# A fused attention and MLP kernel: query transposes of the third batch moved from the DMA engines to TensorE, and a denser order in the first batch

## The chip, the cores and the metric

The kernel runs on one core of one Trainium2 chip. The core has a matrix engine (TensorE, PE in the profile, its weight loads PEld), a vector engine (VectorE, DVE), an activation engine (ScalarE, ACT), a general engine (GpSimd, POOL) and a synchronisation engine (SyncE, SP), and it shares 16 DMA engines among all of its transfers. The metric is the time of one execution on the device in microseconds (us). The kernel before took 806.96 us as the median of three runs (805.3 to 807.57); the execution that was profiled took 805.28 us, of which the profile covers a span of 803.5 us.

## The reference

The reference is grouped attention followed by a residual MLP. Eight batches have 384 positions, 16 query heads, 4 key and value heads and a head size of 64, so that the model width is 1024 and the hidden width 4096.

```python
scores = (1 / 8) * q @ k.T            # per batch and query head, k shared by 4 heads
attn   = softmax(scores)              # over the keys
x      = attn @ v                     # put together as [batch, 384, 1024]
a1     = alpha1 * x + beta1
tok    = w_tok @ a1                   # 384 x 384, mixes positions
u      = x + lam * tok
a2     = alpha2 * u + beta2
out    = u + lam * (relu(a2 @ w_ch1) @ w_ch2)      # 1024 -> 4096 -> 1024
```

All inputs and the output are float32. The kernel rounds what goes through TensorE to bfloat16.

## The kernel before: the parts that matter

The eight batches run as a pipeline. `main(b)` is the MLP of batch b. It has two passes: the first (`h`) computes the hidden layer, 32 blocks of 8 matmuls, and streams the first weight matrix from memory in 16 tiles of two blocks each; the second (`ch`) multiplies by the second weight matrix, which stays on the chip. `side(b + 1)`, the attention and token mixing of the next batch, is woven into the matmuls of `main(b)`, mostly into its second pass. The first batch has nobody's MLP to hide behind: its `side(0)` runs alone at the head of the kernel, in a hand-written order.

Each batch needs its keys and queries turned, with the head dimension on the partitions (`kT`, `qT`). Two means exist for this. A *flip* is a transposing DMA from one on-chip buffer to another. A *turn* is a TensorE transpose into PSUM, and a copy of the result by VectorE.

```python
def flip_queue(b):
    return nc.scalar if b == 2 else nc.sync

def flip_k(b):                                  # 12 blocks of 128 x 128
    flip_queue(b).dma_start_transpose(out=kT..., in_=k2s[b]...)

def flip_q(b, i=0, n=NP):                       # n pairs of heads: 3 n blocks
    flip_queue(b).dma_start_transpose(out=qT[:, i:i + n]..., in_=qrs[b][:, 2 * i:2 * (i + n)]...)
...
def load_w1(n):                                 # one tile of the first weight matrix
    t = sb.tile([P, NDT, CW * P], bf, tag="w1", name="w1", bufs=RING)      # RING = 5
    nc.gpsimd.dma_start(out=t, in_=w1src[...])
...
def q_transpose(p, n=2, tag="tp", eng="DVE"):   # a turn of n pairs: 3 n transposes, one copy
    src = qrs[1][:, 2 * p:2 * (p + n)] if b else qgs[...]
    ps = bank([P, n * NST, P], tag, "tp", src.dtype)
    for i in range(n * NST):
        nc.tensor.matmul(out=ps[:, i, :], lhsT=src[:, i * P:(i + 1) * P], rhs=..., is_transpose=True, ...)
    evac(eng)(out=qT[:, p:p + n]..., in_=ps)
```

Batches are counted from 0, so the third batch is `b == 2`. Its keys and queries are flipped while the first pass of `main(1)` runs, and the flips are issued from ScalarE's queue. All later batches are flipped from SyncE's queue during a second pass. In the first pass ScalarE also empties every second block of hidden units from PSUM (the even `nt`; VectorE takes the odd ones), and TensorE has two PSUM banks for these blocks (tag `mm`).

```python
# main(b), first pass, for each of 16 weight tiles and each of its two blocks nt
ps = bank([P, 512], "mm", "h")                  # two banks in turn
for dt in range(NDT):
    nc.tensor.matmul(out=ps[:, :n], lhsT=w1[:, dt, ...], rhs=a2T[:, dt, :n], ...)
    if dt == 3: yield 0                         # a place where side work may come in
if nt % 2 == 0:
    nc.scalar.activation(out=hT[:, nt, :], in_=ps[:, :S], func=RELU, bias=c1)
else:
    nc.vector.tensor_scalar(out=hT[:, nt, :], in0=ps[:, :S], ...)
yield 0                                         # so two places a block, 64 in the pass
...
load_w1(b * NCH + c + RING)                     # when tile c is used up, tile c + 5 is asked for
```

```python
moves = []                                      # (pass, place, what)
if b == 1:
    moves = [(0, 46 + 4 * i, flip_q, 2, 2 * i - 2, 2) if i else (0, 46, flip_k, 2) for i in range(5)]
```

In the first batch beta1 has to enter the token mixing through a product of two small matrices (`R` and `H`), since the sum `alpha1 * x + beta1` is not formed there. `R` is made of row sums of `w_tok` (`rows_r`), `H` of beta1 times lam, split into three bfloat16 parts so that nothing is lost in rounding (`scale_rows(1)`, `split(1, 2)`, then `fill_h`). All of this runs on VectorE.

```python
def split(lo, hi, step=None):
    for i, m in enumerate(masks[:2]):
        nc.vector.tensor_copy(out=rows_b[:32, c], in_=src[:, c])
        nc.vector.scalar_tensor_tensor(out=dst[:, c], in0=rows_b[:32, c], scalar=m, in1=src[:, c], op0=MUL, op1=subtract)
    nc.vector.tensor_copy(out=rows_b[:32, c], in_=rows_f[:, c])
...
at = {...                                       # after scores(i), for i in 0 to 17
      4: [(av, 0)], 5: [(wtok_transpose, 0, "av"), (wtok_transpose, 1, "tp")],
      6: [(av, 1), (wtok_transpose, 2, "av"), (k_transpose, 2, 2, "tp")],
      7: [(q_transpose, 4, 2, "av"), (scale_rows, 1), (split, 1, 2)],
      8: [(fill_h, 0), (rows_r, "tp"), (av, 2)], 9: [(spread, upper, ...), (q_transpose, 6, 2, "mm")],
      10: [(tok, 0)], 11: [(av, 3)], 12: [(tok, 1), (ut, 0)], 13: [(av, 4), (tok, 2)], ...
```

Here `scores(i)` are the score matmuls, each followed by an exponential on ScalarE; `av(p)` multiplies by the values for head pair p, after which VectorE normalises (a reciprocal and a product into `x`) and multiplies by alpha1 (`a1`); `tok(p)` is the token mixing, `ut(p)` the transpose of u for the MLP. `av`, `tok` and one of the query turns take the two `mm` banks in turn.

Of the kernel before, what the change touches and what calls it, by code (L numbers as in the profile page):

```python
# [12 lines left out]
def kernel(  # L13
# [21 lines left out]
    nc = tc.nc  # L35
    f32 = mybir.dt.float32
# [2 lines left out]
    RELU = mybir.ActivationFunctionType.Relu  # L39
    MUL = mybir.AluOpType.mult  # L40
    ADD = mybir.AluOpType.add

    B, Hq, S, D = q.shape
    Hkv = k.shape[1]
    G = Hq // Hkv
    DM = Hq * D
    DFF = moe_w_ch1.shape[1]
    P = 128
# [65 lines left out]
        for h in range(0, Hq, G):  # L114
            nc.gpsimd.dma_start(out=qrs[b][:, h:h + G], in_=q[b, h:h + G].rearrange("h (p st) d -> p h st d", st=NST))

    def flip_queue(b):
        return nc.scalar if b == 2 else nc.sync

    def flip_k(b):  # L120
        flip_queue(b).dma_start_transpose(out=kT.rearrange("p st h s -> p (st h) s"),
                                    in_=k2s[b].rearrange("p st h a d -> p (st h a d)"))

    def flip_q(b, i=0, n=NP):
        flip_queue(b).dma_start_transpose(out=qT[:, i:i + n].rearrange("p a j s -> p (a j) s"),
                                    in_=qrs[b][:, 2 * i:2 * (i + n)].rearrange("p h st d -> p (h st d)"))

    w1src = moe_w_ch1.rearrange("(dt di) nf -> di dt nf", di=P)
# [12 lines left out]
        nc.gpsimd.dma_start(out=w2[:, r, cs], in_=w2src[:, r, cs])  # L141

    def bank(shape, tag, name, dtype=f32):
        if tag == "mm":
            return mms.tile(shape, dtype, tag="mm", name=name, bufs=2)
        return psum.tile(shape, dtype, tag=tag, name=name, bufs=2 if tag == "sc" else 1)

    def three():
        return threes[0].tile([P, 2, 4, P], f32, tag="sc", name="sc", bufs=3)

    def tp_ps(shape, tag="tp"):
        return bank(shape, tag, "tp", bf)
# [21 lines left out]
    def side(b):  # L174
# [8 lines left out]
        def cols(p):  # L183
            return slice(p * P, (p + 1) * P)

        def bc(t, p):
            return t[:, None, cols(p)].to_broadcast([P, NST, P])
# [7 lines left out]
                                  in_=ps.rearrange("p (h st) s -> p h st s", h=n))  # L195

        def q_transpose(p, n=2, tag="tp", eng="DVE"):
            src = qrs[1][:, 2 * p:2 * (p + n)] if b else qgs[2 * p // G][:, 2 * p % G:2 * p % G + 2 * n]
            src = src.rearrange("p h st d -> p (h st d)")
            f = src.dtype == f32  # L200
            ps = bank([P, n * NST, P], tag, "tp", src.dtype)
            for i in range(n * NST):
                nc.tensor.matmul(out=ps[:, i, :], lhsT=src[:, i * P:(i + 1) * P], rhs=ident_f if f else ident,  # L203
                                 is_transpose=True, start=(i == 0), stop=(i == n * NST - 1), skip_group_check=True)
            evac(eng)(out=qT[:, p:p + n].rearrange("p a j s -> p (a j) s"), in_=ps)
# [33 lines left out]
        def av_piece(p, hh):  # L239
            if hh == 0:  # L240
                if first:
                    avs[p] = bank([P, 2, NST, D1], "mm", "av")
                else:
                    avs[p] = three()[:, 0].rearrange("p k s -> p (k s)")[:, :2 * NST * D1].rearrange(
                        "p (h st d) -> p h st d", h=2, st=NST)
            av = avs[p]
            hk = (2 * p + hh) // G
            for sq in range(NST):
                m = NST * hh + sq
                for sk in range(NST):  # L250
                    k = (p * NST + sk) * NST + m // 2
                    nc.tensor.matmul(out=av[:, hh, sq, :], lhsT=ess[k // 4][:, m % 2, k % 4, :],  # L252
                                     rhs=vb[:, sk, hk, :], start=(sk == 0), stop=(sk == NST - 1))
            if hh == 0:
                return
            rinv = sb.tile([P, 2, NST, 1], f32, tag="rinv", name="rinv", bufs=1)
            nc.vector.reciprocal(out=rinv, in_=av[:, :, :, D:])  # L257
            nc.vector.tensor_tensor(out=x[:, :, cols(p)].rearrange("p st (h d) -> p h st d", h=2), in0=av[:, :, :, :D],  # L258
                                    in1=rinv.to_broadcast([P, 2, NST, D]), op=MUL)
            if first:  # L260
                a1s[p] = hTf[:, 6144 + p % 3 * S:6144 + (p % 3 + 1) * S].rearrange("p (a d) -> p a d", a=NST)
                nc.vector.tensor_tensor(out=a1s[p], in0=x[:, :, cols(p)], in1=bc(g1, p), op=MUL)
                return
            t = sb.tile([P, NST, P], f32, tag="tmp", name="a1f", bufs=4)
            nc.vector.tensor_tensor(out=t, in0=x[:, :, cols(p)], in1=bc(g1, p), op=MUL)  # L265
            a1s[p] = sb.tile([P, NST, P], bf, tag="a1", name="a1", bufs=2)
            nc.vector.tensor_tensor(out=a1s[p], in0=t, in1=bc(h1, p), op=ADD)  # L267

        def tok(p):
            ps = bank([P, NST, P], "mm", "tok") if first else three()[:, 0, :NST]  # L270
# [78 lines left out]

        if not first:  # L350

            turns = {}
            if b == 1:
                turns = {4: [(split, 2, 4, 0)], 8: [(split, 2, 4, 1)], 12: [(k_transpose, 0)],
                         16: [(q_transpose, 0, 2, "av")], 20: [(k_transpose, 2)]}
                for i in range(3):
                    turns[24 + 4 * i] = [(q_transpose, 2 + 2 * i, 2, "av")]
                for i in range(4):
                    turns[34 + 4 * i] = [(spread, (2 * i, 2 * i + 1), (1, 3), "tp", "ACT")]
                for i in range(2):  # L360
                    turns[50 + 4 * i] = [(spread, range(4 * i, 4 * i + 4), (3, 4), "av", "ACT")]
            return turns, {
                0: [(scores3, 0)], 4: [(av, 0)], 6: [(scores3, 1)], 8: [(tok_flip, 0)], 11: [(av, 1)],
                13: [(scores3, 2, True)], 15: [(av, 2)], 16: [(tok_flip, 1)], 18: [(tok_flip, 2)], 19: [(av, 3)],
                21: [(scores3, 3)], 23: [(tok_flip, 3)], 25: [(av, 4)], 27: [(scores3, 4)], 29: [(tok_flip, 4)],
                31: [(av, 5)], 33: [(scores3, 5, True)], 35: [(av, 6), (tok_flip, 5)], 37: [(av, 7)],
                39: [(tok_flip, 6)], 41: [(tok_flip, 7)]}
# [5 lines left out]
        ut = a2_transpose  # L373
        at = {0: [(warmup, 3), (scale_rows, 0), (split, 0, 1, 0)], 1: [(k_transpose, 1, 1), (split, 0, 1, 1)],
              2: [(q_transpose, 2, 2, "av")], 3: [(warmup, 1), (spread, lower, (0, 1), "tp")],
              4: [(av, 0)], 5: [(wtok_transpose, 0, "av"), (wtok_transpose, 1, "tp")],
              6: [(av, 1), (wtok_transpose, 2, "av"), (k_transpose, 2, 2, "tp")], 7: [(q_transpose, 4, 2, "av"), (scale_rows, 1), (split, 1, 2)],
              8: [(fill_h, 0), (rows_r, "tp"), (av, 2)], 9: [(spread, upper, (0, 1), "av", "ACT"), (q_transpose, 6, 2, "mm")],
              10: [(tok, 0)],
              11: [(av, 3)], 12: [(tok, 1), (ut, 0)], 13: [(av, 4), (tok, 2)], 14: [(ut, 1), (fill_h, 4), (tok, 3)],  # L380
              15: [(av, 5), (ut, 2)], 16: [(tok, 4), (ut, 3)], 17: [(av, 6), (tok, 5)]}
        for i in range(18):
            add(scores, i)
            for f, *a in at.get(i, []):
                add(f, *a)
        for f, *a in ((ut, 4), (h_part, (0, 1), range(4)), (av, 7), (ut, 5), (tok, 6),
                      (h_part, (2, 3), range(4)), (h_part, range(4), (4,)), (ut, 6), (tok, 7),
                      (h_part, range(4), (5,)), (ut, 7), (h_part, range(4), (6,)), (h_part, range(4), (7,))):
            add(f, *a)
        return us  # L390
# [64 lines left out]
    with tc.manual_schedule(engines=order):  # L455
# [59 lines left out]
                nc.vector.tensor_reduce(out=t[:n], in_=ident[:n, :n].rearrange("p (k c) -> p c k", c=NP), op=ADD, axis=AX)  # L515


        def scale_rows(i):
            r = rows_f[:, i * P:(i + 1) * P]
            nc.vector.tensor_tensor(out=r, in0=r, in1=rows_f[:, 3 * P:4 * P], op=MUL)  # L520


        def split(lo, hi, step=None):
            c = slice(lo * P, hi * P)
            for i, m in enumerate(masks[:2]):
                if step in (None, i):
                    src, dst = (rows_t, rows_f) if i else (rows_f, rows_t)
                    nc.vector.tensor_copy(out=rows_b[:32, c], in_=src[:, c])
                    nc.vector.scalar_tensor_tensor(out=dst[:, c], in0=rows_b[:32, c], scalar=m, in1=src[:, c],
                                                   op0=MUL, op1=mybir.AluOpType.subtract)  # L530
            if step != 0:
                nc.vector.tensor_copy(out=rows_b[:32, c], in_=rows_f[:, c])


        def fill_h(p):
# [2 lines left out]
                                    in1=sel4[:, p:p + 4, None].to_broadcast([32, 4, P]), op=MUL)  # L538

        load_v(0)  # L540
        nc.gpsimd.dma_start(out=wtok_in, in_=moe_w_tok.rearrange("(p tt) s -> p tt s", tt=NST))
        load_q4(2)
        load_q4(3)
        place_k(0, 0, (0,))
        for c in range(RING):
            load_w1(c)
        place_k(0, 1)

        load_k(1)
        load_q(1)  # L550
# [7 lines left out]
        load_k(2)  # L558
        for b in range(B):
            us = side(b + 1) if b + 1 < B else ({}, {})  # L560


            moves = []
            if b == 1:
                moves = [(0, 46 + 4 * i, flip_q, 2, 2 * i - 2, 2) if i else (0, 46, flip_k, 2) for i in range(5)]
            if 0 < b < B - 2:
                moves += [(1, 1, load_k, b + 2), (1, 2, load_next, b + 2), (1, 34, flip_k, b + 2), (1, 36, flip_q, b + 2, 0, 2),
                          (1, 37, flip_q, b + 2, 2, 2), (1, 42, flip_q, b + 2, 4, 2), (1, 43, flip_q, b + 2, 6, 2)]
# [38 lines left out]
```

The softmax here doesn't subtract the row's maximum and nothing guards it: scores larger than these inputs give would overflow.

## Time and profile before

The profile is that of one execution. Idle time of an engine counts only if it holds up the engine that sets the end.

| What | Before |
|---|---|
| time, median of three runs | 806.96 us (805.3 to 807.57) |
| profiled span | 803.5 us |
| VectorE busy | 343.5 us (43%) |
| ScalarE busy | 226.9 us (28%) |
| GpSimd busy | 178.5 us (22%), 112.1 us of it in issuing the w_ch1 loads |
| tiles of w_ch1, issue to landing | 128, 512 KB each |
| flips of queries on ScalarE's queue | 4, 13.0 us from issue to landing |
| flips of queries on SyncE's queue | 20, 2.8 us from issue to landing (median) |

A line of the timeline gives the start and the length of a group of instructions, the engine, the line of the kernel, what is written and read with its shape, the number of instructions, and in square brackets the time for which the engine stood idle before it and what ended that wait. Engine letters with a q (ACTq, SPq) are the engine's sequencer, which issues DMAs. Lengths of neighbouring matmuls overlap, because they are pipelined; how long a piece of TensorE work really takes is read from the distance between starts.

### The profile page before, as it was taken

Reading aid. Unit: us, or ns where it says so; the run is one execution under the profiler, and the core shown is the slowest. Engines: PE = TensorE matmul, PEld = TensorE weight load, DVE = VectorE, ACT = ScalarE, POOL = GpSimd, SP = SyncE. Lnnn points to the kernel's source line nnn. Section 1 sums busy time; section 2 is a strip of 40 time slices with the busy share of each in tenths; the row PEclk is TensorE's granted clock in tenths of the full one; section 3 lists DMA queues with packets and bytes.
Section 4 is the critical chain, followed back from the end, with each engine's and each line's share of the span. In section 5 each row is a group of like instructions: output and inputs, shape, how many; then the busy total and the mean of one; then the engine's idle time right before and its main releaser. Section 6 shows DMA issues by size and latency. Waiting matters only on the chain.

```text
span 803.5 us, 14220 instructions
## 1 busy us (share of the span) xinstructions
PE 793.8 (99%) x6123; PEld 452.0 (56%) x6123; DVE 343.5 (43%) x669; ACT 226.9 (28%) x309; POOL 178.5 (22%) x233
## 2 busy tenths in 40 slices
PE   8999999999999999999999999999999999999997
PEld 4766555655556555565555655566555655556545
DVE  8652465215552266322662236622366225552122
ACT  6624431223402233123221233122431223312100
POOL 7234231332013500135002340033400330003000
PEclk9999999999999999999999999999999999999999
DMA  9999999999269972999439991499914995129611
GB/s 190 202 186 202 205 207 170 187 186 170 66 126 188 198 101 58 162 189 196 74 73 169 193 196 43 92 174 197 163 46 114 165 198 88 48 61 187 82 40 40
DMA packets 234975, 113.17 MB, mean 141 GB/s; under 512 B 84376, under 2 KB 228768, under 8 KB 234912
## 3 DMA queue, kind: packets, MB, share of 16 engines
q0 software_dynamic: 170752, 83.47, 79.1%
q1 hardware_dynamic: 58848, 27.22, 13.5%
q10 hardware_dynamic: 5312, 1.57, 1.5%
q8 instruction: 48, 0.79, 0.4%
q14 instruction: 15, 0.12, 0.0%
HBM read 170.53 MB, written 12.58 MB: 228 GB/s over the span
## 4 chain that ended last, share of the span: by engine, by line
PE 84%; DMA 10%; issue 3%; DVE 1%; POOL 1%; ACT 0%; POOLq 0%
PE ch L443 37%; PE h L410 34%; DMA w<-in_moe_w_ch_dram 8%; PE sc L217 4%; PE sc L252 3%; PE sc L273 3%; DMA qT<-q_raw 1%; POOL w L136 1%; PE h L168 1%; PE tok L273 1%; PE av L252 0%; PE warm L460 0%; PE ut L290 0%; PE tp L203 0%; ACT hT L226 0%
## 5 line engine op out<-in xcount | busy, mean ns | idle before, releaser
L443 PE MATMUL ch<-w,hT 128*128 128x512 bf16 (+2 forms) x1600 | 357.7, 371 | 1.1 <-DVE o L448 0.9
L410 PE MATMUL h<-a2T,w 128*128 128x384 bf16 (+1 forms) x2016 | 331.5, 326 | 0.8 <-ACT hT L418 0.8
L410 PEld LDWEIGHTS <-w 128*128 128x128 bf16 x2016 | 196.8, 98 | 131.2 <-issue 1.5
L443 PEld LDWEIGHTS <-hT 128*128 128x128 bf16 x1600 | 144.6, 98 | 153.1 <-issue 10.5
L136 POOL DMA_DIRECT2D w<-in_moe_w_ch_dram x128 | 112.1, 878 | 519.3 <-PE h L410 500.5
L226 ACT ACTIVATE es<-sc 128x1024 bf16<-128x1024 f32 x126 | 121.4, 1023 | 187.9 <-PE sc L217 175.8
L420 DVE TENSOR_SCALAR hT<-h,bias 128x384 bf16<-128x384 f32 x128 | 79.1, 618 | 218.3 <-PE h L410 217.7
L418 ACT ACTIVATE hT<-h,bias 128x384 bf16<-128x384 f32 x128 | 74.3, 580 | 304.9 <-PE h L410 299.4
L448 DVE TENSOR_TENSOR o<-ch,vecs 128x512 f32<-128x512 f32 (+2 forms) x50 | 33.4, 669 | 107.8 <-PE ch L443 107.8
L252 PEld LDWEIGHTS <-es 128*128 128x128 bf16 x1008 | 38.2, 97 | 13.2
L273 PEld LDWEIGHTS <-wtokT 128*128 128x128 bf16 x576 | 37.3, 98 | 13.8 <-DVE x L258 1.7
L217 PE MATMUL sc<-qT,kT 64*128 64x384 bf16 (+2 forms) x576 | 41.9, 272 | 0.7 <-DMA qT<-q_raw 0.6
L257 DVE RECIPROCAL rinv<-sc 128x6 f32<-128x6 f32 x56 | 10.8, 193 | 68.4 <-PE sc L252 67.5
L252 PE MATMUL sc<-v,es 128*128 128x65 bf16 x1008 | 39.9, 193 | 0.0
L280 DVE TENSOR_TENSOR x<-sc,x 128x384 f32<-128x384 f32 x56 | 31.0, 553 | 20.0 <-PE sc L273 20.0
L273 PE MATMUL sc<-a,wtokT 128*128 128x128 bf16 x504 | 37.3, 219 | 0.0
L217 PEld LDWEIGHTS <-kT 64*128 64x128 bf16 x576 | 21.6, 94 | 24.5 <-issue 18.2
L449 DVE TENSOR_TENSOR o<-o,x 128x512 f32<-128x512 f32 (+2 forms) x50 | 33.5, 670 | 1.7
L284 DVE TENSOR_TENSOR a<-x,vecs 128x384 bf16<-128x384 f32 x56 | 32.7, 584 | 1.9
L265 DVE TENSOR_TENSOR a1f<-x,vecs 128x384 f32<-128x384 f32 x56 | 31.2, 558 | 1.9
L267 DVE TENSOR_TENSOR a<-a1f,vecs 128x384 bf16<-128x384 f32 x56 | 31.2, 558 | 1.9
L258 DVE TENSOR_TENSOR x<-sc,rinv 128x384 f32<-128x384 f32 x56 | 31.2, 558 | 1.9
(75 smaller groups left out, 203.1 us busy)
## 6 DMA issues: line engine op xcount, KB each, us to landing
w<-in_moe_w_ch_dram POOLq DMA_DIRECT2D x144, 512.0 KB, 8.6
out_dram<-o SPq DMA_DIRECT2D x47, 256.0 KB, 2.0
q_raw<-in_q_dram POOLq DMA_DIRECT2D x28, 192.0 KB, 8.1
kst<-in_k_dram SPq DMA_DIRECT2D x16, 192.0 KB, 3.4
v<-in_v_dram POOLq DMA_DIRECT2D x24, 64.0 KB, 7.9
a2T<-a SPq DMA_TRANSPOSE x56, 2.3
qg<-in_q_dram POOLq DMA_DIRECT2D x3, 192.0 KB, 5.9
stage<-in_q_dram ACTq DMA_DIRECT2D x2, 192.0 KB, 3.7
```

The costliest lines, as they stand in the source:

```text
L136: nc.gpsimd.dma_start(out=t, in_=w1src[:, :, c * CW * P:(c + 1) * CW * P])
L217: nc.tensor.matmul(out=sc[:, hh, k % 4:k % 4 + n], lhsT=kT[r, sk, 2 * p // G, :], rhs=qT[r, p, st:st + n, :], start=True, stop=True)
L226: nc.scalar.activation(out=e, in_=sc, func=EXP, scale=scale_qk)
L252: nc.tensor.matmul(out=av[:, hh, sq, :], lhsT=ess[k // 4][:, m % 2, k % 4, :], rhs=vb[:, sk, hk, :], start=(sk == 0), stop=(sk == NST - 1))
L273: nc.tensor.matmul(out=ps[:, tt, :], lhsT=wtokT[:, st, tt * P:(tt + 1) * P], rhs=a1s[p][:, st, :], start=(st == 0), stop=(st == NST - 1 an ...
L284: nc.vector.tensor_tensor(out=a2s[p], in0=u, in1=bc(al2, p), op=MUL)
L410: nc.tensor.matmul(out=ps[:, :n], lhsT=w1[:, dt, j * P:(j + 1) * P], rhs=a2T[:, dt, :n], start=(dt == 0), stop=(dt == NDT - 1))
L418: nc.scalar.activation(out=hT[:, nt, :], in_=ps[:, :S], func=RELU, bias=c1)
L420: nc.vector.tensor_scalar(out=hT[:, nt, :], in0=ps[:, :S], scalar1=c1, scalar2=0.0, op0=ADD, op1=mybir.AluOpType.max)
L443: nc.tensor.matmul(out=ps[:, lo:hi], lhsT=hT[:, nt, ms * P:(ms + 1) * P], rhs=w2[:, nt, dw * 512 + lo:dw * 512 + hi], start=(nt == 0), sto ...
L448: nc.vector.tensor_tensor(out=o[:, lo:hi], in0=ps[:, lo:hi], in1=lam_t[:, c], op=MUL)
L449: nc.vector.tensor_tensor(out=o[:, lo:hi], in0=o[:, lo:hi], in1=x[:, ms, c], op=ADD)
```

## The change

There are two parts. The first concerns the third batch. The flips that went through ScalarE's queue are gone. The keys and the first two of the eight query pairs are now flipped from SyncE's queue at the head of the first pass of `main(1)`; the other six pairs are turned by TensorE at three places in the same pass, in PSUM banks that are unused then, and copied by VectorE. The aim is to take work out of ScalarE's instruction stream and to halve what the transposing DMAs move while weights are being streamed.

The second part concerns the first batch. The scaling and splitting of beta1 goes from VectorE to GpSimd, which does it between two of its weight loads (eight small instructions where VectorE had six, because the fused multiply and subtract becomes two). The product with alpha1 is a step of its own, `a1`, that can stand later than the normalisation. The transposes of `w_tok` and the first token mixings stand later in the order, more of the attention stands before them, and the loads of the third query group and of `w_tok` change places. The aim is that TensorE, which works through the order strictly, finds less often that what it needs is still being made.

```diff
-    def flip_queue(b):
-        return nc.scalar if b == 2 else nc.sync
     def flip_k(b):
-        flip_queue(b).dma_start_transpose(...)
+        nc.sync.dma_start_transpose(...)
     def flip_q(b, i=0, n=NP):
-        flip_queue(b).dma_start_transpose(...)
+        nc.sync.dma_start_transpose(...)
...
-            turns = {}
+            turns = {16 + 8 * i: [(q_transpose, 2 + 2 * i, 2, "three")] for i in range(3)} if b == 2 else {}
...
-                moves = [(0, 46 + 4 * i, flip_q, 2, 2 * i - 2, 2) if i else (0, 46, flip_k, 2) for i in range(5)]
+            moves = [(0, 1, flip_k, 2), (0, 1, flip_q, 2, 0, 2)] if b == 1 else []
...
-              4: [(av, 0)], 5: [(wtok_transpose, 0, "av"), (wtok_transpose, 1, "tp")],
-              6: [(av, 1), (wtok_transpose, 2, "av"), (k_transpose, 2, 2, "tp")], 7: [(q_transpose, 4, 2, "av"), (scale_rows, 1), (split, 1, 2)],
-              8: [(fill_h, 0), (rows_r, "tp"), (av, 2)], 9: [(spread, upper, (0, 1), "av", "ACT"), (q_transpose, 6, 2, "mm")],
-              10: [(tok, 0)],
-              11: [(av, 3)], 12: [(tok, 1), (ut, 0)], 13: [(av, 4), (tok, 2)], 14: [(ut, 1), (fill_h, 4), (tok, 3)],
-              15: [(av, 5), (ut, 2)], 16: [(tok, 4), (ut, 3)], 17: [(av, 6), (tok, 5)]}
+              4: [(av, 0)], 5: [(a1, 0)], 6: [(av, 1), (k_transpose, 2, 2, "tp")],
+              7: [(q_transpose, 4, 2, "av"), (a1, 1)], 8: [(av, 2)],
+              9: [(wtok_transpose, 0, "av"), (wtok_transpose, 1, "tp")],
+              10: [(wtok_transpose, 2, "av"), (q_transpose, 6, 2, "mm"), (fill_h, 0)], 11: [(av, 3), (rows_r, "tp")],
+              12: [(spread, upper, (0, 1), "av"), (a1, 2)], 13: [(tok, 0), (av, 4), (a1, 3)],
+              14: [(tok, 1), (ut, 0), (a1, 4)], 15: [(av, 5), (tok, 2), (a1, 5), (fill_h, 4)], 16: [(ut, 1), (tok, 3)],
+              17: [(ut, 2), (av, 6), (a1, 6)]}
...
-        for f, *a in ((ut, 4), (h_part, (0, 1), range(4)), (av, 7), (ut, 5), (tok, 6),
-                      (h_part, (2, 3), range(4)), (h_part, range(4), (4,)), (ut, 6), (tok, 7),
+        for f, *a in ((tok, 4), (ut, 3), (h_part, (0, 1), range(3)), (av, 7), (a1, 7), (tok, 5), (ut, 4), (h_part, (0, 1), (3,)),
+                      (tok, 6), (h_part, (2, 3), range(4)), (ut, 5), (tok, 7), (h_part, range(4), (4,)), (ut, 6),
                       (h_part, range(4), (5,)), (ut, 7), (h_part, range(4), (6,)), (h_part, range(4), (7,))):
...
         load_v(0)
+        load_q4(2)
         nc.gpsimd.dma_start(out=wtok_in, ...)
-        load_q4(2)
         load_q4(3)
         place_k(0, 0, (0,))
-        for c in range(RING):
+        load_w1(0)
+        load_w1(1)
+        place_k(0, 1)
+        scale_rows(1, nc.gpsimd)
+        split(1, 2, None, nc.gpsimd)
+        for c in range(2, RING):
             load_w1(c)
-        place_k(0, 1)
```

## The prediction

> **What bounds the kernel now.** I read the page first, for what is full and when.
>
> ```profile
> PE 793.8 (99%) x6123; PEld 452.0 (56%) x6123; DVE 343.5 (43%) x669; ACT 226.9 (28%) x309; POOL 178.5 (22%) x233
> ...
> PE   8999999999999999999999999999999999999997
> PEclk9999999999999999999999999999999999999999
> DMA  9999999999269972999439991499914995129611
> ```
>
> TensorE is busy 793.8 of 803.5 us at full granted clock, and its pieces really stream: between flips and turns, 16 matmuls of a first pass take 2.61 us from start to start, 163 ns for 384 columns. So the most that better order can give is the 9.7 us in which TensorE is idle, and each matmul added costs its full time. The DMA row says that the engines are full for the first fifth of the span, to about 200 us: both parts of the change lie there. Next I read TensorE's waits.
>
> ```profile
> PE warm L460 <- DVE wtokT L463: 1.5, 1, 1.5
> PE tok L273 <- DVE x L258: 1.4, 1, 1.4
> PE ch L443 <- DVE o L448: 0.9, 2, 0.5
> PE h L410 <- ACT hT L418: 0.8, 3, 0.4
> PE sc L217 <- DMA qT<-q_raw: 0.6, 1, 0.6
> PE tp L203 <- DVE wtokT L305: 0.4, 1, 0.4
> PE ch L443 <- ACT hT L418: 0.2, 1, 0.2
> PE tp L192 <- POOL k L106: 0.2, 1, 0.2
> ```
>
> This is nearly all that can be won. The first line is the start of the kernel and the third its end; neither is touched. The timeline puts the others in two places. In the first batch: 0.22 us at 12.66, 0.44 at 13.93, 1.43 at 18.96, together **2.09 us**. At the end of the second batch's first pass: 0.19 at 167.60, 0.23 at 170.59, 0.41 at 173.77, 0.23 at 176.75, 0.64 at 178.42, together **1.70 us**. VectorE's timeline shows the cause of the first group:
>
> ```profile
> 14.94 0.27 DVE L520 TENSOR_TENSOR hT<-hT 32x128 f32<-32x128 f32 x1
> ...
> 16.61 0.21 DVE L532 CAST hT<-hT 32x128 bf16<-32x128 f32 x1
> 16.86 0.68 DVE L536 TENSOR_TENSOR stage<-hT,stage 32x512 bf16<-32x512 bf16 x1
> ...
> 18.35 0.56 DVE L258 TENSOR_TENSOR x<-av,rinv 128x384 f32<-128x384 f32 x1
> ```
>
> Scaling and splitting beta1 holds VectorE from 14.94 to 16.86; the normalisation of pair 2, whose values TensorE had finished by 16.2, comes only at 18.35, and the first `tok` needs the bank that it empties. ScalarE's timeline shows the cause of the second:
>
> ```profile
> 163.78 3.14 ACTq L121 DMA_TRANSPOSE kT<-k  x1
> 166.97 0.58 ACT L418 ACTIVATE hT<-h,bias 128x384 bf16<-128x384 f32 x1 [2.85 <-PE h L410]
> 166.99 2.92 ACTq L125 DMA_TRANSPOSE qT<-q_raw  x1
> 169.96 0.58 ACT L418 ACTIVATE hT<-h,bias 128x384 bf16<-128x384 f32 x1 [2.41 <-PE h L410]
> ```
>
> Each flip keeps ScalarE's sequencer 2.9 to 3.7 us, more than the 2.60 us between two of its blocks, so emptying the bank comes late and TensorE waits.
>
> **What the Trainium skill says.** Four places bear on this. "DMA: Bandwidth & Descriptors", section "Issuing engines are not separate DMA queues": DMAs issued from different engines run on the same 16 engines and interleave, so another queue saves only the issuing sequencer's time. The trace agrees: with the flips in flight the weight tiles issued at 159.90 and 173.65 landed at 167.84 and 189.83, 7.9 and 16.2 us after issue. Moving flips to SyncE therefore frees ScalarE, but not the DMA engines. "TensorE: Matmul & The Clock Gate", Part 4, PE-mode transpose: a transpose ends in PSUM and needs a VectorE copy; it gives about 275 ns for one in a kernel's context. Here six of them push the next matmul back by only 0.34 us (the earlier turns: 47.30 to 47.64), so I use that. "GPSIMD Engine Reference", 3.1: an elementwise float32 instruction is about 1.96 times slower there than on VectorE. The trace of before has no such arithmetic on GpSimd, only copies, so it can't confirm this. "SBUF — State Buffer", "Who interferes with whom": a GpSimd instruction and a VectorE copy in a two-port mode, or one with two inputs in SBUF, can block each other for a whole instruction. A hint of it is in the trace: GpSimd's copies of 128x384 take 500 to 512 ns as a rule, but up to 837 ns.
>
> **Part 1, the third batch.**
> - Removed: the four waits for ScalarE and the one for the flipped q, −1.70 us. In the new order the last query copy is done some 20 us before the scores of batch 2 ask for it.
> - Added: three turns of six transposes, 3 × 0.34 = **+1.02 us** on TensorE. Their copies are 3 × 0.56 us on VectorE, which has one 0.62 us block every 2.60 us there: beside other work. The query loads that they read landed by about 131 us and the first turn comes near 144, so they wait for nothing; the PSUM banks they use are idle in a first pass.
> - Moved: the flips of k and two q pairs, now at about 135.5 instead of 163.8 to 176. Counting a group of six blocks as a unit, six units were flipped before and three are now. In before, six units made the weight tile issued at 173.65 land some 8.6 us later than the 2.67 us pace of the tiles before would have (167.84 + 5 × 2.67 = 181.2, against 189.83): 1.4 us a unit, so 4.3 us for three. They start while the DMA engines are idle (share 0.00 from 134 to 135 us), which saves 1 to 1.5 us, so the tiles of this pass will land about **3 us later** than before (2.5 to 4.2).
> - Slack for this: comparing first use and landing of each tile, tile 5 had 3.9 us, tiles 6 to 8 2.7 to 2.8, tiles 9 to 12 2.3 to 2.1. Each turn ahead of a tile adds 0.34: 3.1 to 3.4 us from tile 6 on. So 3 us just fits; 4.2 would not, and would cost 1.1. I charge **+0.3 us**.
> - Sum: −1.70 + 1.02 + 0.3 = −0.4 us.
>
> **Part 2, the first batch.** I laid the new order of TensorE and VectorE along the durations of the trace before. It starts alike to 10.6 us, where the scores come to wait for the exponentials, one each 0.93 us. The k transpose no longer waits: GpSimd casts at about 9 instead of 11.4 us. `scores` 6 to 9 and `av` 1 and 2 follow closely to 14.3; then come the three w_tok transposes, of which the third waits for the first one's copy (VectorE first finishes pair 2): about 0.4 us. The first `tok` comes near 19.0 as before, and needs nothing late: its bank was emptied, and R is ready near 18.9. The second waits some 0.3 us for the addition that empties its bank. After that I find no wait. What differs is what lies behind: when the second `tok` begins, near 21.0 in both, TensorE has also done two `scores` (2 × 0.33) and one `av` (0.66). That is 1.3 us ahead; in waits, 2.09 − 0.7 = 1.4. I take **−1.4 us**.
> GpSimd: six VectorE instructions took 1.92 us; at the ratio of the skill, and as eight, I estimate 4 to 5 us, so done at 14 to 15 us; `fill_h` asks for it at 16.8. Tiles 2 to 4 of the weights are issued some 5 us later, but DMA is behind anyway: tile 1 landed only at 19.43 although issued at 7.96.
> Will being early be lost again to DMA? Tile 5 of the first batch landed 1.0 us before its use, the last slice of the second weight 1.1 us. Tile 5 is asked for when the first tile is used up, so it moves along, and the engines are slack from 39 to 42 us (119 to 183 GB/s for 2 us, about 195 later), worth 0.8 us. So 1.0 − 1.4 + 0.8 = 0.4 us is left. I charge **+0.1**.
>
> **Sum.** −0.4 − 1.3 = −1.7 us: the profiled span from 803.5 to about 801.8, the median from 806.96 to 805.3 us, 0.2%.
>
> **Rivals.**
> 1. *The flips at the head starve the weights.* For it: tile landings are paced at 2.64 to 2.70 us by full DMA queues while TensorE asks for one each 2.60, so a delay isn't made good within the pass, and the loads of the next k now queue behind the flips. Against: half the transposed bytes, and an idle DMA at the start. If all 4.3 us and the k loads count, TensorE waits 1.5 to 2 us on `w` tiles and part 1 loses 1: about 806.5.
> 2. *GpSimd is late with beta1.* Blocked by VectorE's, its instructions could take 1 us each; `fill_h` then holds VectorE, in strict order, and a wait of 1 to 2 us returns in front of `tok`. Against: 2 us of slack, and only 32 partitions by 128 elements. Time: 806.5.
> 3. *DMA takes the gain back in the first batch*, because weights arrive on their own clock until 130 us: the 1.4 us show up again as waits for tile 5 or for the last slices of w2. Time: 806.4.
> 4. *All goes better*: no wait for tiles and 2.0 us won at the head: 804.3.
>
> **Range and chances.** The terms that are sure, 3.8 us of waits and 1.0 us of transposes, bound the best case at 2.8 us won. Rivals 1 to 3 each take about a microsecond. The three runs before spread 2.3 us themselves, as much as the effect. So 803.5 to 807.3 us should hold it 8 times in 10. Two per cent is 16 us, which no term here comes near.
>
> **What would show it.** Right: TensorE's wait list has no line for the ScalarE eviction L418 or for qT; 18 transposes more, each group 0.34 us; the stretch from start to the first full `h` block 1.4 us shorter; wait of the first `tok` gone, about 0.7 us left in small ones. Wrong: TensorE waits for `w` in the second or first batch's `h`, VectorE waits for GpSimd at `fill_h`, or new waits among the first batch's `tok` beyond 1 us.

## The result, and the profile after

The changed kernel took 804.12 us as the median of four runs (803.92 to 804.36), beside 806.14 us for the kernel before: a ratio of 0.9973, with a 95% interval of 0.9955 to 0.9991. In a second comparison it took 803.69 us beside 806.37 (39 runs of before): 0.9970 (0.9958 to 0.9981). So 2.0 to 2.7 us are won, a little more than the 1.7 predicted, and the time lies inside the range. Both parts were mis-sized, though, and the experiments show how. The page of the profile after, its busy times and its rows by slice:

```profile
PE 790.1 (98%) x6074; PEld 454.0 (57%) x6141; DVE 344.1 (43%) x667; ACT 226.6 (28%) x308; POOL 182.2 (23%) x241
...
PE   8999999999999999999999999999999999999997
PEclk9999999999999999999999999999999999999999
DMA  9999999998279962999339991499914994139511
```

Nothing has moved at this scale; the 18 new weight loads stand in PEld (6141 for 6123; some matmul records are missing in this trace, so PE's count is no guide). What moved is in TensorE's waits (engine, line, what it waited for, us in total, times, longest):

```profile
PE warm L464 <- DVE wtokT L467: 1.5, 1, 1.5
PE ch L447 <- issue: 1.1, 7, 0.2
PE ch L447 <- DVE o L452: 0.9, 2, 0.5
PE vec L332 <- DVE hT L540: 0.6, 1, 0.6
PE h L414 <- DMA a2T<-a: 0.4, 1, 0.4
```

All five waits that the change aims at are gone: ScalarE's L418, the flipped q, the first `tok`, the query turn behind w_tok, the k transpose. Two new ones are there. The first spread (a small product, L332, that hands the split rows of the scale vectors to all partitions) waits for the split row on VectorE, and the head of the second batch's `h` pass waits for a transpose of a2. ScalarE's timeline in that pass is now even, with 2.02 us of rest between two evictions where a flip stood before:

```profile
164.54 0.58 ACT L422 ACTIVATE hT<-h,bias 128x384 bf16<-128x384 f32 x1 [2.02 <-PE h L414]
167.14 0.58 ACT L422 ACTIVATE hT<-h,bias 128x384 bf16<-128x384 f32 x1 [2.02 <-PE h L414]
```

And this is TensorE's timeline in the same pass, with the three turns (0.33 to 0.34 us from start to start) and the new wait in front:

```profile
132.66 1.14 PE L414 MATMUL h<-a2T,w 128*128 128x384 bf16 x6
134.16 10.48 PE L414 MATMUL h<-a2T,w 128*128 128x384 bf16 x62 [0.36 <-DMA a2T<-a]
144.48 0.50 PE L203 MATMUL tp<-ident,q_raw 128*128 128x128 bf16 x6
144.81 5.36 PE L414 MATMUL h<-a2T,w 128*128 128x384 bf16 x32
...
176.99 0.83 PE L217 MATMUL sc<-qT,kT 64*128 64x384 bf16 x12
```

From the timelines I read two marks in every trace below. *Mark 1* is the first matmul of the first batch's `h` pass proper (38.48 us before, 37.70 after): how long the lone first batch takes. *Mark 2* is the first score matmul of batch 2 (178.42 before, 176.99 after). The distance between them, 139.94 before and 139.29 after, holds the third batch's flips or turns, and every wait for weights on the way. Past mark 2 all kernels run alike to within 0.5 us.

### The profile page after: what moved, and what is told of

The parts are those of the page before. It is cut to its first block, busy times and chain, and to the rows that moved or that the text cites. A ratio compares the mean times of both kernels' runs of the same rounds, so it can differ in the third digit from the quotient of the medians.

```text
span 802.3 us, 14186 instructions
## 1 busy us (share of the span) xinstructions
PE 790.1 (98%) x6074; PEld 454.0 (57%) x6141; DVE 344.1 (43%) x667; ACT 226.6 (28%) x308; POOL 182.2 (23%) x241
## 4 chain that ended last, share of the span: by engine, by line
PE 96%; DVE 2%; issue 1%; DMA 1%; ACT 0%; SPq 0%
PE h L414 41%; PE ch L447 40%; PE sc L217 4%; PE sc L252 4%; PE sc L275 3%; DMA a2T<-a 1%; PE h L168 1%; PE tp L203 1%; PE tok L275 0%; PE av L252 0%; PE warm L464 0%; PE ut L292 0%; DVE x L258 0%; DVE x L282 0%; PE vec L332 0%
## 5 line engine op out<-in xcount | busy, mean ns | idle before, releaser
L447 PE MATMUL ch<-w,hT 128*128 128x512 bf16 (+2 forms) x1533 | 346.1, 370 | 4.4 <-issue 1.1
```

Source lines behind the costliest of these rows:

```text
L447: nc.tensor.matmul(out=ps[:, lo:hi], lhsT=hT[:, nt, ms * P:(ms + 1) * P], rhs=w2[:, nt, dw * 512 + lo:dw * 512 + hi], start=(nt == 0), sto ...
```

## The experiments

**The two parts apart.** The comparison of the two traces suggested a first theory of mine that fell: the first batch was 0.78 us early at mark 1 and at tile 1 of the second batch's `h` pass, after the wait for a2T, exactly level with before (136.03 against 136.04), so that all the gain seemed to be part 1. `p1_only` is the kernel before with the third batch's edit, `p2_only` the change with that edit undone:

```diff
# p2_only, against the change
-            turns = {16 + 8 * i: [(q_transpose, 2 + 2 * i, 2, "three")] ...} if b == 2 else {}
+            turns = {}
-            moves = [(0, 1, flip_k, 2), (0, 1, flip_q, 2, 0, 2)] if b == 1 else []
+            # flips of batch 2 from ScalarE at places 46 to 62, as before
```

> The kernel before with part 1 alone (third batch). Theory A, from comparing the traces: the whole gain of the change is part 1, since removing the five late waits is worth 2.46 us by distance of starts (not the 1.70 that the idle times add up to), against 1.0 us of turns: time 1.2 to 1.7 us below before, from tile 1 of the second batch's h pass to the first score of batch 2 about 40.9 us (before: 136.04 to 178.42, 42.4 us). Theory B, as predicted: part 1 is worth 0.4 us only.

> The change with part 1 undone, so part 2 alone (first batch). Theory A: the first batch ends 0.8 to 1.6 us earlier than before (38.48 us), but TensorE then waits for the transposes of a2 (flips that land late among the q and v loads) at the head of the second batch's h pass, so tile 1 of that pass is used near 136.0 us as before, and the time is within 0.4 us of before. Theory B, as predicted: the gain of 1.3 us is kept to the end.

Measured: part 1 alone 805.68 us (806.56 before), ratio 0.9989 (0.9982 to 0.9995), so 0.9 us won; part 2 alone 804.46 us, ratio 0.9974 (0.9963 to 0.9984), so 2.1 us won. The theory "all is part 1" is refuted: it allowed part 2 no more than 0.4 us. The prediction's shares (0.4 and 1.3) lie at the low ends of the two intervals, which reach from 0.4 to 1.5 and from 1.3 to 3.0 us. The trace of `p1_only` shows why two profiles alone misled: its first batch is the old one, and mark 1 came at 40.10 us, not at 38.48. VectorE there, and GpSimd beside it:

```profile
8.32 1.50 DVE L527 CAST hT<-hT 32x128 bf16<-32x128 f32 x1
9.85 0.34 DVE L528 SCALAR_TENSOR_TENSOR hT<-hT,stage 32x128 f32<-32x128 bf16 x1
```

```profile
7.08 4.44 POOL L133 DMA_DIRECT2D w<-in_moe_w_ch_dram  x5
```

The same cast took 0.25 us in the profile that the prediction read. While it ran, GpSimd was issuing weight loads. So the old first batch isn't one number.

**How much the first batch varies.** `before_again` is the kernel before, `after_again` the change, both untouched.

> The kernel before once more, for the end of the first batch. In two executions with that same first batch it came at 38.48 (before) and 40.10 us (part 1 alone), where in the second a VectorE cast took 1.50 instead of 0.25 us beside GpSimd's issue of weight loads. Theory A, the old order is at the mercy of such blocks: the end lies between 38.4 and 40.5 us, with a cast or a split instruction above 0.6 us where it is late. Theory B, 40.10 was an exception: 38.4 to 38.7 us.

> The change once more, for its time against before and for the end of the first batch. With that first batch it came at 37.70, 37.70, 37.69 and once at 36.55 us; the old one at 38.48, 39.68 and 40.10. Theory A, the old order varies and was lucky in the profile that the prediction read (mean 39.4), so that the change is worth 2.0 to 2.8 us: time 803.5 to 804.3. Theory B: 1.6 us as predicted, 804.7 or more.

Measured: mark 1 of the old first batch now came at 39.68 us; of the new at 37.70 again. Over all traces the old one gives 38.48, 39.68, 40.10 (mean 39.4), the new one 37.70, 37.70, 37.70, 37.69 and 36.55 (mean 37.5). The difference, 1.9 us, fits what part 2 alone won. In `before_again` another instruction was hit, while GpSimd cast k:

```profile
11.54 1.36 DVE L262 TENSOR_TENSOR hT<-x,vecs 128x384 bf16<-128x384 f32 x1
```

```profile
11.42 1.06 POOL L106 CAST k<-kst 128x384 bf16<-128x384 f32 x2
```

This product takes 0.56 us elsewhere. The delay moved the whole chain behind it: a w_tok transpose waited 0.3 us, the query turn behind it 0.7 and the first `tok` 1.5. Another 0.4 us went to the landing of w_tok itself. The second trace of the change had no wait for a2T; it waited for a weight tile instead (0.2 us at 162.66).

Much of this variation goes with something that I had overlooked: how fast TensorE opens. Its first matmuls take longer than all later ones (a warm-up matmul of 384 columns 527 ns at first, 326 ns afterwards), and the moment at which this ends differs between executions of the same instructions. Here is the same stretch in the trace of before and in the first trace of the change:

```profile
4.83 1.16 PE L203 MATMUL tp<-hT,stage 128*128 128x128 f32 x6
5.92 0.39 PE L217 MATMUL sc<-qT,kT 64*128 64x384 bf16 x4
```

```profile
4.81 1.56 PE L203 MATMUL tp<-hT,stage 128*128 128x128 f32 x6
6.31 0.61 PE L217 MATMUL sc<-qT,kT 64*128 64x384 bf16 x4
```

The start of the first score matmul (6.31 in the last line) tells an early opening from a late one. All traces, those of the experiments below included:

| First batch | Run | First score (us) | Mark 1 (us) |
|---|---|---|---|
| old | `before` | 5.92 | 38.48 |
| old | `before_again` | 6.12 | 39.68 |
| old | `p1_only` | 6.42 | 40.10 |
| old, beta1 on GpSimd | `gps_only` | 6.17 | 38.76 |
| new, beta1 on VectorE | `beta_on_dve` | 6.32 | 38.96 |
| new | `all_flips_head` | 5.99 | 36.55 |
| new | `p2_only`, `v_later` | 6.20 | 37.70, 37.69 |
| new | the change, `after_again` | 6.31, 6.30 | 37.70 |
| new, k cast later | `k_cast_later` | 5.81 | 36.45 |
| new, k cast later | `combo`, `k3_late` | 6.18, 6.38 | 37.15, 37.14 |
| new, GpSimd held | `quiet` | 5.84 | 36.38 |

Within each order an early opening has the early mark 1. The lines of VectorE give a path for it: its split of the first row stands behind copies that wait for TensorE's transposes, so a late opening moves the split against GpSimd's work. (`before_again` is another case: its first spread started at 9.05 us, like before's at 9.00, and its delay is the one told above.) No run sets the opening, so this is a correlation and not an experiment. Compared at like openings, the new order is 1.9 us earlier (36.55 against 38.48) or 2.0 to 2.4 us (37.70 against 39.68 and 40.10).

**What in part 2 does it.** `gps_only` is the old order with beta1 on GpSimd, which also moves GpSimd's cast of k forward as in the change; `beta_on_dve` the new order with beta1 on VectorE, where it stands behind the third query turn.

```diff
# gps_only, against the kernel before
-   7: [(q_transpose, 4, 2, "av"), (scale_rows, 1), (split, 1, 2)],
+   7: [(q_transpose, 4, 2, "av")],          # and scaled and split on GpSimd after weight tile 1
# beta_on_dve, against the change
-        scale_rows(1, nc.gpsimd)
-        split(1, 2, None, nc.gpsimd)
-   7: [(q_transpose, 4, 2, "av"), (a1, 1)],
+   7: [(q_transpose, 4, 2, "av"), (a1, 1), (scale_rows, 1), (split, 1, 2)],
```

> The kernel before with beta1's scaling and splitting on GpSimd, in the change's order of GpSimd, everything else as before. Theory A, the 1.9 us of VectorE are what held up the first token mixing: its wait (1.3 to 1.5 us) falls below 0.4 us, the first batch ends 1.0 to 1.5 us earlier than before's 38.5 to 40.1, time 805.0 to 805.6. Theory B, the order matters more than the engine: less than 0.6 us won.

> The change with beta1's scaling and splitting back on VectorE, behind the copy of the third query turn, the rest of the change kept. Theory A, VectorE's 1.9 us matter in the new order too: the w_tok transposes and the first token mixing wait for it, 1 to 1.6 us more than in the change (first batch ends at 38.6 to 39.3), time 0.8 to 1.5 us above the change. Theory B, the new order has room for it: within 0.4 us of the change.

Measured: `gps_only` 805.61 us, ratio 0.9992 (0.9985 to 0.9998), 0.8 us won; mark 1 at 38.76. The wait of the first `tok` fell to 0.2 us as expected, but two others stayed: 0.7 us behind w_tok, and 1.2 us for the first spread. `beta_on_dve` (which also holds part 1) 805.72 us, ratio 0.9996 (0.9987 to 1.0004), which can't be told from before; mark 1 at 38.96. There the 1.9 us of VectorE came back as one wait, in the second line of its wait list:

```profile
PE tp L304 <- DVE wtokT L307: 1.7, 1, 1.7
PE warm L464 <- DVE wtokT L467: 1.5, 1, 1.5
```

Four of its 13 runs (806.08 to 808.07 us) had a granted clock of 0.996 or 0.997; the median of the other nine is 805.35, about 1.0 us below before, which part 1 alone would give. So neither half of part 2 wins the 2.1 us alone: beta1 on GpSimd gives 0.8, the order by itself nothing that these runs can tell from part 1. That each half needs the other (VectorE's time is of use only where TensorE has something to do meanwhile, and the other way round) is how I read it.

**The block between GpSimd and VectorE.** In four of the five traces of the new first batch the second fused subtract of VectorE's own split took 1.02 us, and the first spread waited 0.6 to 1.2 us for that split. GpSimd was casting k just then:

```profile
8.99 1.02 DVE L534 SCALAR_TENSOR_TENSOR hT<-hT,stage 32x128 f32<-32x128 bf16 x1
```

```profile
8.84 1.03 POOL L107 CAST k<-kst 128x384 bf16<-128x384 f32 x2
```

A cast of the same split had taken 0.72 to 0.86 us in these four traces already, while GpSimd issued weight loads. In the fifth trace (`all_flips_head`, below), the one with the early opening, VectorE was through that subtract at 8.60, before the cast began; no instruction of its split took over 0.47 us, and mark 1 came at 36.55. The change itself moved that cast from 11.4 to 8.8 us. `k_cast_later` puts four weight loads ahead of it instead of two:

```diff
-        load_w1(0)
-        load_w1(1)
+        for c in range(4):
+            load_w1(c)
         place_k(0, 1)
...
-        for c in range(2, RING):
+        for c in range(4, RING):
```

> The change, with GpSimd casting the second half of k and splitting beta1 after four weight loads instead of two, so some 1.8 us later, when VectorE is through its own split. Theory A: the 0.58 us wait of the first spread (its input rows come late because a VectorE instruction took 1.02 instead of 0.34 us beside GpSimd's cast) goes, and the first batch ends 0.4 to 0.6 us earlier than 37.70; whether the time follows depends on the wait for the flips of a2 at the head of the next pass: if that takes it back, the time is unchanged within 0.2 us. Theory B: VectorE's slow instructions come from the weight loads' issue and not from the cast, and the wait stays.

Measured: 803.40 us (803.35 to 804.15), ratio 0.9963 (0.9950 to 0.9977). The fused subtract took 0.47 us, the spread waited 0.2, mark 1 came at 36.45, 1.25 us earlier than in the change. Not all of this is the cast's doing, for this trace had an early opening: against `all_flips_head`, with an early one too, it is 0.10 us ahead, and `combo` and `k3_late`, with this order on GpSimd and late openings, are 0.55 ahead of the change. In those two the fused subtract took 0.34 and 0.48 us, but a cast of the split took 0.90 and 0.77 beside the issue of weight loads. So both theories hold in part. Of the 1.25 us only 0.66 are left at mark 2 (176.33 against 176.99): the wait list of this trace has 0.8 us for `w` tiles, at 45.30 (first batch) and at 162.22.

`quiet` goes further. It keeps the change's order on GpSimd, but lets GpSimd wait, by one tiny copy, until VectorE has split its row, and has the late k loads of `k3_late`, which is described below:

```diff
+        def gps_rest():
+            nc.gpsimd.tensor_copy(out=stage[:32, 2860:2861], in_=rows_b[:32, 0:1])
+            # then GpSimd's weight loads, cast, beta1 as in the change, and the first loads of batch 1 and of w2
...
-              2: [(q_transpose, 2, 2, "av")],
+              2: [(gps_rest,), (q_transpose, 2, 2, "av")],
```

> As the version with the late load of the fourth batch's keys, but with the change's order on GpSimd, which is held by one tiny copy until VectorE has split the first row (about 8.6 us); so GpSimd neither issues nor casts while VectorE does so. Theory A, VectorE's slow instructions of 7 to 10 us come from GpSimd working at the same time: none is above 0.5 us there, the first spread waits under 0.1 us, and the first batch ends at 36.0 to 36.5 us (with the cast merely later: 36.45 to 37.15); time 0.3 to 0.8 us below 802.9. Theory B, they come from something else (loads landing, ScalarE): the wait of the first spread stays at 0.2 to 0.6 us.

Measured: no VectorE instruction of the split above 0.47 us, no wait of the spread, mark 1 at 36.38, as theory A has it. That is less of a proof than it seems: the opening was early here too, and `all_flips_head` has no instruction of the split above 0.47 us either, with GpSimd not held. The time was not as expected: 804.24 us, ratio 0.9982 (0.9970 to 0.9993), 1.3 us above `k3_late`. Holding GpSimd held everything behind it too (the first weight load was issued at 8.79 instead of 7.10), and TensorE waited at tile 5:

```profile
42.60 2.12 PE L414 MATMUL h<-a2T,w 128*128 128x385 bf16 x12
46.03 0.83 PE L414 MATMUL h<-a2T,w 128*128 128x385 bf16 x4 [1.30 <-DMA w<-in_moe_w_ch_dram]
```

**Where earliness goes: the loads.** Two experiments ask whether the flips and loads at the head of the second batch's `h` pass hold up the weights. `all_flips_head` drops the turns and flips everything there. `v_later` loads the third batch's values after weight tile 15 of that pass is asked for.

```diff
# all_flips_head, against the change
-            turns = {16 + 8 * i: ...} if b == 2 else {}
-            moves = [(0, 1, flip_k, 2), (0, 1, flip_q, 2, 0, 2)] if b == 1 else []
+            turns = {}
+            moves = [(0, 1, flip_k, 2)] + [(0, 1, flip_q, 2, 2 * i, 2) for i in range(4)] if b == 1 else []
# v_later, against the change
         load_q(b)
-        load_v(b)
+        if b > 2: load_v(b)
...
+            if b == 1 and c == 10: load_v(2)      # behind load_w1 of tile 15
```

> The change, but with k and all eight query pairs flipped from SyncE at the head of the second batch's h pass, and no turn by TensorE (1.0 us of it saved). Theory A, the flips at the head starve the weights: three more groups of six blocks delay the weight tiles by some 3 to 4 us more, TensorE waits 2 to 4 us for w in that pass, and the time is 1 to 3 us above the change. Theory B, the flips hide in idle DMA time: no wait for w, and the time is 1 us below the change.

> The change, with the values of the third batch (192 KB) loaded in the second batch's h pass after its tile 15 is asked for, instead of right behind the queries at the end of the first batch. If the flips of a2 are late because of the backlog of loads that ends near 134 us (theory A), the wait of 0.4 to 0.8 us at the head of that h pass goes and the time falls by 0.6 to 0.9 us against the change. If the flips are late for a reason of their own (theory B: their inputs or their own issue), the wait stays and the time is that of the change.

Measured: `all_flips_head` 808.41 us, ratio 1.0024 (1.0016 to 1.0032), slower than before although it saves 1.0 us of TensorE and had an early mark 1. The first line of its waits says why, and it is the largest in any of these traces:

```profile
PE h L414 <- DMA w<-in_moe_w_ch_dram: 3.6, 4, 2.1
```

From mark 1 to mark 2 it needs 144.14 us. The rival that flips at the head starve the weights is right in kind; the six pairs turned by TensorE are what keeps it small. `v_later` 804.23 us, ratio 0.9968 (0.9955 to 0.9980), the time of the change (804.12, 803.69): half of its theory holds. The wait for a2T is gone, but 0.5 us for `w` at 162.93 stands in its place, and the distance from mark 1 to mark 2 is 139.40 (139.29 and 138.98 in the change). The backlog was shifted, not removed.

**Less to load ahead of need.** The loads of the next batches' keys stand in front of weight tiles by nothing but SyncE's free running: it issues them as soon as it gets there (in the change those of the fourth batch at 137.91 us, right behind the flips). `k3_late` is `k_cast_later` with the fourth batch's keys issued from ScalarE at place 54 of that pass; `combo` adds the late values and the third batch's keys at place 44 of the first batch's pass.

```diff
# k3_late
-                moves += [(1, 1, load_k, b + 2), ...
+                if b == 1: moves.append((0, 54, load_k, 3, (0, 2), nc.scalar))
+                else:      moves.append((1, 1, load_k, b + 2))
# combo, in addition
-        load_k(2)
+            moves = ... if b == 1 else [(0, 44, load_k, 2, (0, 2), nc.scalar)] if b == 0 else []
```

> The change with the later cast on GpSimd (as in k_cast_later), and with the keys of the fourth batch (384 KB) loaded at the end of the second batch's h pass from ScalarE's queue instead of right behind the flips at its head. Theory A, flips and k loads together push the weight tiles late: tiles 5 to 15 land about 2 us earlier before their use than in k_cast_later, its waits for w at tile 6, 11 and 12 to 15 (0.6 us between tile 1 and the first score of batch 2: 41.58 against 40.96 us without any) go, and the time falls by 0.5 us against k_cast_later. Theory B, the flips alone do it: the waits stay within 0.2 us of what they were.

> The change with the later cast on GpSimd, the values of the third batch loaded late, and the keys of the third and fourth batch loaded late from ScalarE's queue (at the ends of the first and of the second batch's h pass). If all that the first batch gains is taken back by loads that stand ahead of what TensorE needs next (theory A), no wait for w or a2T above 0.2 us is left before 180 us, the first score of batch 2 comes near 175.0 us (k_cast_later: 176.33, the change: 176.99) and the time is 1.0 to 1.5 us below k_cast_later. If the backlog is in the weights themselves (theory B), waits for w come back further on and the time stays within 0.5 us of k_cast_later.

Measured: `k3_late` 802.91 us, ratio 0.9955 (0.9941 to 0.9969); `combo` 802.79 us, ratio 0.9956 (0.9944 to 0.9969). In both, no wait for `w` or a2T is left up to mark 2. The wait list of `k3_late`:

```profile
PE warm L464 <- DVE wtokT L467: 1.5, 1, 1.5
PE ch L447 <- DVE o L452: 0.9, 2, 0.5
PE vec L332 <- DVE hT L540: 0.4, 1, 0.4
PE sc L217 <- ACT qT L205: 0.2, 1, 0.2
```

From mark 1 to mark 2 they need 138.53 and 138.58 us. That is the distance without waits, so the change (139.29, 138.98) still spent 0.5 to 0.8 us on loads, and `k_cast_later` (139.88) 1.3. Only half of these 1.3 us are the keys' doing: the second batch's `h` pass takes 42.60 us in `k3_late` (132.11 to 174.71) and 43.24 in `k_cast_later` (132.13 to 175.37). The other half is the wait for tile 5 of the first batch, 90 us before these keys are loaded. Mark 1 came 0.7 us later in `k3_late`, at 37.14, TensorE did not wait for tile 5, and behind it the two traces are level (46.31 and 46.30 us): the earlier first batch had won nothing. Against `k_cast_later` 0.5 and 0.6 us of the time are won, and 0.2 and 0.3 us of the distance to before (806.56 us beside `k_cast_later`, 806.27 beside these). So `k3_late` met its expectation in the waits, and in the time (0.5 us) if the two times are compared directly; `combo` fell short of the 1.0 to 1.5 us expected, having nothing left to win on this stretch. Both have lower medians than either kernel.

## Why the prediction was right, point by point

The total was right (805.3 predicted, 804.12 and 803.69 measured, 803.5 to 807.3 as range), and the waits that it names did go. That the number comes so close is in part luck. It stands on a before of 806.96 us, where later medians are 806.14 to 806.56. And in the two profiles part 1 gave more than its 0.4 us (0.65) and part 2 less than its 1.3 (0.78), while over all traces both gave more.

- *"Removed: ... −1.70 us."* The mechanism was right and the size too small. I added up the printed idle times. The printed ends of matmuls overlap the next one's start, so part of a stall hides in the matmul before it: at 173.77 the idle time was 0.41 us, but the distance from the previous weight tile, 170.59, is 3.18 us instead of 2.60. By distances, the last four tiles of before's pass (164.64 to 176.75) cost 12.11 us for 10.40, and 1.67 from there to mark 2 for 0.96: 2.4 us in all.
- *"3 × 0.34 = +1.02 us."* Right: 144.48 to 144.81, 150.01 to 150.35, 155.55 to 155.88.
- *"I charge +0.3 us"* for weights behind the flips. The step under it was mis-sized: up to the one that before asked for at 159.90, the tiles of that pass landed 1.1 to 1.5 us later than in before in the change's first trace and 2.0 to 2.7 in `after_again`, not 3. Yet the charge was too small, since TensorE came to the pass 0.8 us earlier: the change waited 0.5 (tiles) and 0.8 us (a2T) longer than the 138.5 us without waits, `p1_only` 0.3. With the old handling of the third batch the distance was 139.94, 140.32, 140.48 and 140.04 us (mean 140.2), with the new one 138.86, 139.29, 138.98, 139.40 and 139.33 (mean 139.2). So part 1 is worth 1.0 us, where 0.4 was predicted: the term that was mis-sized is the first, 2.4 us instead of 1.70.
- *"I take −1.4 us"* for the first batch. *"It starts alike to 10.6 us"* did not come true in the change's traces. The profile that I laid the new order upon was a lucky one, with an early opening and mark 1 at 38.48, where two other traces of that order have 39.68 and 40.10. In the change's first trace the first spread, at 9.00 in before, came at 10.46. The new order's end was foretold 1.4 us earlier, near 37.1, and came at 37.70, so −0.8 against the profile read, but −1.9 against the mean and, in `all_flips_head`, −1.9 at a like opening. So behind the opening the order won more than foretold. The third w_tok transpose and the second `tok` waited 0.05 and 0.13 us rather than 0.4 and 0.3.
- *GpSimd's part.* Foretold 4 to 5 us, done at 14 to 15; it ran from 9.76 to 13.93, with instructions of 0.28 to 0.60 us, and `fill_h` at 17.78 didn't wait for it. The Trainium skill's ratio, applied to 1.92 us, served well: a product of 32x128 took 0.45 to 0.57 us on GpSimd and 0.27 on VectorE. The second rival ("GpSimd is late with beta1") is refuted as stated. But the mechanism under it, which the Trainium skill describes in "SBUF — State Buffer", section "Who interferes with whom", struck elsewhere: not beta1 held VectorE up, but, where the opening was late, the cast of k that the change had moved forward (a fused subtract, which has two inputs in SBUF, took 1.02 us instead of 0.34). I had counted that move as gain alone.
- *The third rival*, that loads take back what the first batch wins, holds in part: tile 5 of the first batch kept 0.6 us (0.4 foretold) in the change, and turned into a wait of 0.5 us in `k_cast_later`, whose first batch was 1.25 us faster.

Open is how the share of the two parts adds up: alone they won 0.9 and 2.1 us, together 2.0 and 2.7 in two comparisons, with intervals wide enough for a plain sum. The waits for loads speak for some loss, without measuring it.

## What to carry to other kernels

Judge a stall by the distance between starts, not by the idle time printed, when the engine's ends are modelled. When a stretch hangs on strict order between engines that can block each other, one profile is a draw from a spread: read two or three of the old kernel before laying a new order upon one, find where they first part, and compare new and old traces that start alike. And where an engine is 99% busy and its data stream is paced like itself, a faster head is worth only what the loads behind it let through, so look at what is loaded before it is needed.

## What was not expected of the hardware

VectorE instructions of 0.25 to 0.56 us took 1.02 to 1.50 us while GpSimd cast a tile or issued loads, and between executions of the same instructions the end of the first batch moved by up to 1.6 us. How much of that is GpSimd's blocking and how much TensorE's opening isn't separated. And with three groups of six blocks more among the transposing DMAs, 0.2 us of waiting for weights (`after_again`) became 3.6 us, in a trace whose first batch ended 1.15 us earlier. TensorE's slow opening is over by 4.66 us in before, and in the first profile of the change it still reaches into the second warm-up, whose three matmuls took 0.86 us from the first one's start to the next score (6.85 to 7.71), where before has 0.59 (6.25 to 6.84), at a granted clock that both pages show as full; why its end differs is open.
